# Attention by steps of two query tiles, with the score matmuls of two heads in the two halves of TensorE's rows

## The chip, the cores and the metric

One core of one Trainium2 chip runs the whole program. The metric is the device time of one execution in microseconds, and the time before is the median of 3 runs. TensorE (PE in the profile; PEld is its loading of weights) multiplies, VectorE (DVE), ScalarE (ACT) and GpSimd (POOL) do the elementwise work, and SyncE (SP) issues the DMAs.

## What is computed

Inputs are q, k and v of shape (4, 8, 576, 64): four batches, eight heads, 576 positions, 64 dimensions a head. A small network makes a bias from the distance of two positions. Attention is followed by two MLPs over 2304 tokens.

```python
scores = scale * np.matmul(q, k.transpose(0, 1, 3, 2))
x = (np.log1p(np.abs(rel)) / np.log1p(np.maximum(pos[:, None], 1.0)))[..., None]
bias = np.maximum(x @ w1 + b1, 0.0) @ w2
scores = scores + bias.transpose(2, 0, 1)[None, :, :, :]
scores = scores - np.max(scores, axis=-1, keepdims=True)
attn = np.exp(scores)
attn = attn / (np.sum(attn, axis=-1, keepdims=True) + 1e-09)
out = np.matmul(attn, v)
...
g = h - np.tanh(h)
...
(gate * val) @ w_out
```

## The kernel before

The program has three stages that overlap at their seams: the bias (`bias_phase`, lines 28 to 94), attention (`attention_phase`, lines 127 to 400) and the MLPs (`mlps`, lines 549 to 768). All instructions are put in order by hand: each engine runs its own in the order in which the program's loops emit them.

**Attention** runs over 16 units, a unit being a pair of heads of one batch. A unit has nine query tiles of 128 rows. Tiles 0 to 7 are four blocks of 128 queries, each once for the first head (even tile) and once for the second (odd tile); tile 8 holds the last 64 queries of both heads. The loop at line 333 makes one turn for each tile and works on several tiles at once, at fixed lags: scores of tile t (lag 0), `reduce_min` (lag 1), `expo` (lag 2), `norm` (lag 5), `transposes` (lag 7), `settle` and `settle5` (lag 8).

- `scores` (line 220) multiplies queries with keys. To keep float32 accuracy with the fast format fp32r, each operand is split into a high and a low part. The queries' high part stands in partitions 0 to 63 and their low part in 64 to 127 (`qs`); the keys' high part is there twice, in both halves (`kh`), and their low part likewise (`kl`). So one matmul over all 128 rows gives (qh+ql)·kh and a second (qh+ql)·kl. A tile has 576 scores in each row, in two halves of 288, so it takes four matmuls of 288 columns (line 231). Tile 8 needs both heads' keys and takes ten, since the second head's keys are stored rolled by 64 positions and one half is put together from a piece of 224 and one of 64 columns (`PIECES`, line 122).
- `reduce_min` (line 234, DVE) adds the bias, flips the sign and takes the minimum of each row; it frees the PSUM buffer that `scores` filled. There are two such buffers (line 211), one tile in each.
- `expo` (line 250, ACT) is the exponential with the row's sum, `stats` (line 255, DVE) the reciprocals, `norm` (line 261, POOL) the division.
- `transposes` (line 265, PE) turns a tile by four 128x128 transposes (line 273), with one more for every odd tile (line 277) and, for tile 8, two small matmuls on 64 rows and 64 columns each (lines 281 and 282). `settle` and `settle5` (lines 296 to 308) copy the results to SBUF.
- `pv_steps` (line 310) multiplies with the values for a group of four or five tiles, 256 or 320 columns wide: first two full matmuls (line 320), then sixteen that write 64 output columns of the array each, two heads side by side (line 323). A float32 matmul runs as two instructions. `PV_BURST` (line 404) spreads a group over two of the loop's turns.
- The operands are made by `load_raw`, `high` and `low` (lines 153 to 189): for each unit four raw tiles (queries and keys, each head in a tile of its own, loaded into both partition halves by two DMAs), three casts on ACT and one on DVE, four subtractions and one clearing on POOL. `HIGH` and `LOW` say at which turn.
- `filler` (line 809) puts conversions of the first MLP's weights between, by the table `KIND`; `tail` (line 819) starts the MLPs at the turns in `AT`, counted from the end of the last unit.

In a turn TensorE gets its instructions in this order: the scores of one tile (line 367), the steps of `pv_steps` that are due (lines 371 to 377), the transposes of an earlier tile (line 383). The same functions as the diff touches them follow.

Of the kernel before, what the change touches and what calls it, by code (L numbers as in the profile page):

```python
# [12 lines left out]
ALU = mybir.AluOpType  # L13
# [110 lines left out]
ON_ACT5 = (1, 3, 5, 8)  # L124


def attention_phase(tc, qT, kT, vP, ident_d, par, c_log, bsc, xs, after_bias, load_weight, filler, tail):

# [3 lines left out]
    with ExitStack() as st, ExitStack() as early:  # L132
        right = lambda n, k: st.enter_context(tc.tile_pool(name=n, bufs=k, side="right"))
        vp, np_, sm, xp = right("p1v", 4), right("p1n", NBUF), right("p1m", 3), right("p1x", 2)
# [31 lines left out]
        def alloc(u):  # L166
            prep[u] = (qp.tile([128, 2 * S + 64], F32R, name="qs"), qp.tile([128, 2, S], F32R, name="kh"),
                       qp.tile([128, 2, S], F32R, name="kl"))

        def high(u, i):  # L170
            qs, kh, kl = prep[u]
            a = i // 2
            o = kh[:, a] if i % 2 else qs[:, a * (S + 64):a * (S + 64) + S]
            if i == 3:
                V.tensor_copy(o, raws[u, i])
            else:
                A.copy(o, raws[u, i])

        def low(u, i):
            qs, kh, kl = prep[u]  # L180
            a = i // 2
            r = raws.pop((u, i))
            if i % 2 == 0:
                w = qs[64:128, a * (S + 64):a * (S + 64) + S]
                G.tensor_sub(w, r[64:128], w.bitcast(F32))
                if a == 0:
                    G.memset(qs[:, S:S + 64].bitcast(F32), 0.0)
            else:
                G.tensor_sub(kl[:, a], r, kh[:, a].bitcast(F32))

        def during(k):
            if k < 0:
                alloc(0)
                for i in range(4):
                    load_raw(0, i)
                load_v(0)
                nc.sync.dma_start(ident, ident_d)
            elif 6 <= k < 14 and k % 2 == 0:
                high(0, k // 2 - 3)
            elif 6 <= k < 14:  # L200
                low(0, k // 2 - 3)
# [18 lines left out]
        def scores(u, t):  # L220
            qs, kh, kl = prep[u]
            s = ps_s.tile([128, 2, 512], F32, name="sc")
            if t == 8:
                ops = [(a, qs[:, o:o + 128], k_) for a, o in ((0, 512), (1, S)) for k_ in (kh, kl)]
            else:
                o = t // 2 * 128 + t % 2 * (S + 128)
                ops = [(t % 2, qs[:, o:o + 128], k_) for k_ in (kh, kl)]
            for i, (a, w, k_) in enumerate(ops):
                for hf in range(2):
                    for x, y, n in PIECES[hf] if t == 8 and a else ((0, 288 * hf, 288),):  # L230
                        T.matmul(s[:, hf, x:x + n], w, k_[:, a, y:y + n], start=(i == 0), stop=(i == len(ops) - 1 and x + n == S // 2))  # L231
            sc[u, t] = s

        def reduce_min(u, t):
            s = sc.pop((u, t))
            if t == 8:
                n = np_.tile([128, S], F32, name="n8", bufs=1)
            else:
                if t % 2 == 0:
                    npair[u, t // 2] = np_.tile([128, 2 * S], F32, name="n")  # L240
                n = npair[u, t // 2][:, S * (t % 2):S * (t % 2) + S]
            if t % 3 == 0:
                nmin[u, t // 3] = sm.tile([128, 3], F32, name="mn")
                nsum[u, t // 3] = sm.tile([128, 3], F32, name="sums")
            m = nmin[u, t // 3][:, t % 3:t % 3 + 1]
            V.tensor_tensor_reduce(n.rearrange("p (a b) -> p a b", a=2), s[:, :, 0:288],  # L246
                                   bias[t].rearrange("p (a b) -> p a b", a=2), -0.125, 3.0e38, ALU.add, ALU.min, m)
            ntile[u, t] = n

        def expo(u, t):  # L250
            n = ntile[u, t]
            m = nmin[u, t // 3][:, t % 3:t % 3 + 1]
            A.activation(n, n, AF.Exp, bias=m, scale=-1.0, accum_out=nsum[u, t // 3][:, t % 3:t % 3 + 1])  # L253

        def stats(u, g):
            r = sm.tile([128, 3], F32, name="rec")
            V.tensor_scalar(r, nsum[u, g], 1e-9, None, ALU.add)
            V.reciprocal(r, r)
            nrec[u, g] = r

        def norm(u, t):
            n = ntile[u, t]
            G.tensor_scalar(n, n, nrec[u, t // 3][:, t % 3:t % 3 + 1], 1.0, ALU.mult, ALU.mult)  # L263
# [68 lines left out]
        pvq, late, pv_turn = [], [], 9  # L332
        for tau in range(NU * 9 + TAIL):
            u, t = divmod(tau, 9)
            for _ in range(PER[min(tau, len(PER) - 1)]):
                next(bias_steps, None)
            if tau == LAG - 1:
# [5 lines left out]
            def at_lag(lag):  # L343
                z = tau - lag
                return divmod(z, 9) if 0 <= z < NU * 9 else None
            y = at_lag(2)
            if y:
                expo(*y)
# [3 lines left out]
            y = at_lag(LAG - 2)  # L352
            if y:
                if y[1] % 3 == 0:
                    stats(y[0], y[1] // 3)
                norm(*y)
            z = at_lag(LAG + 1)
            if z:
                settle5(*z)
            y = at_lag(1)  # L360
            if y:
                reduce_min(*y)
                hp, b = units[y[0]]
                if b == NB - 1 and hp + 1 < NP:
                    load_bias(hp + 1, y[1])
            if tau < NU * 9:
                scores(u, t)
            if z:
                settle(*z)
            pv_turn += 1  # L370
            for _ in range(PV_BURST.get(pv_turn, 0)):
                if pvq:
                    f = pvq.pop(0)
                    if f.__name__ == "evac":
                        late.append(f)
                        break
                    f()
            if z and z[1] in (3, 8):
                pvq += pv_steps(z[0], z[1] // 8)
                pv_turn = 0  # L380
            y = at_lag(LAG)
            if y:
                transposes(*y)
            if t == 0 and u + 1 < NU:
                alloc(u + 1)
            if t == 6 and u + 1 < NU:
                load_v(u + 1)
            for n, i in ((u + 1, HIGH.get(t)), (u, HIGH.get(t + 9))):
                if i is not None and 1 <= n < NU:
                    high(n, i)  # L390
            for n, i in ((u + 1, LOW.get(t)), (u, LOW.get(t + 9))):
                if i is not None and 1 <= n < NU:
                    low(n, i)
                    if n + 1 < NU:
                        load_raw(n + 1, i)
            if tau < NU * 9:
                filler(t)
            if tau == NU * 9:
                early.close()
            tail(tau - NU * 9)  # L400


TAIL = 16
PV_BURST = {1: 3, 3: 3}
NBUF = 5
EBUF = 4
LR = (16, 19, 22, 25)
# [3 lines left out]
PER = (2, 2, 2, 2, 2, 2)  # L411
TR = 0
ANY = {t: "AVG" for t in range(9)}
AT = (-4, 1, 3, 7)
KIND = {0: "VV", 2: "V", 4: "VV", 6: "AG", 7: "AG", 8: "AG"}
# [368 lines left out]
def tile_attention_then_two_mlps(ctx: ExitStack, tc: tile.TileContext, qT, kT, vP, par, wi, wo, wg, wv, wo2, c_log, ident, out, xs=None):  # L784
# [6 lines left out]
    with tc.manual_schedule():  # L791
# [17 lines left out]
        def filler(t):  # L809
            for k in KIND.get(t, ""):  # L810
                if not held and W.done < EARLY:
# [29 lines left out]
def _layout(inputs):  # L841
# [6 lines left out]
    def roll(x):  # L848
        return np.concatenate([x[:, :, :64], np.concatenate([x[:, :, 64:, 512:], x[:, :, 64:, :512]], axis=3)], axis=2)
    qt, kt = roll(heads(q)), roll(heads(k))  # L850
# [34 lines left out]
```

## Time and profile before

| | |
|---|---|
| median of 3 runs | 1212.06 us (1210.6 to 1214.28) |
| the profiled execution's own time | 1213.29 us |
| its span in the profile | 1211.5 us |
| TensorE busy | 1181.9 us, 98% of the span |
| DVE, ACT, POOL busy | 725.4, 632.0 and 559.8 us |
| mean granted clock of TensorE | 0.994 of full speed |

The profile is of one execution; its span is the time between its first and its last instruction. In a timeline row the first number is the start in us from the span's start and the second the duration; consecutive instructions of one kind are merged into one row with their count (x4). Matmuls overlap, and their recorded ends are modelled, so what one costs is read from the distance of starts. A form such as 128\*64 gives the rows and columns of the array that a matmul uses; 128x288 behind it is what it writes.

### The profile page before, as it was taken

To read this page: it belongs to the slowest core of one execution; us is meant where nothing else is said; L and a number is where in the kernel's file an instruction comes from. 1 tells how busy PE (TensorE), PEld (TensorE's weight loads), DVE (VectorE), ACT (ScalarE), POOL (GpSimd) and SP (SyncE) were. 2 spreads that over 40 slices of the span, in tenths; PEclk is the share of its full clock that TensorE was granted. 3 is DMA by queue.
4 is the path that set the end of the run, shared out by engine and by line. 5 is a ranking of instruction groups with operands and counts; after the bars stand their busy time and mean duration, and the time that the engine had idled before them with its cause. 6 is when DMAs were issued, how large, how long until landed. Compare 5 with 4: busy or idle time off the path is not lost.

```text
span 1211.5 us, 19227 instructions
## 1 busy us (share of the span) xinstructions
PE 1181.9 (98%) x6992; PEld 1044.7 (86%) x6992; DVE 725.4 (60%) x1253; ACT 632.0 (52%) x1257; POOL 559.8 (46%) x536
## 2 busy tenths in 40 slices
PE   7889999999989999999999999999999999999998
PEld 2247777777769999999999999999999999999997
DVE  7888899999839898898988668862001010010100
ACT  6887888888747767677666556332211211111111
POOL 1039889899735555565555334452221212112111
PEclk9999999999989999999999999999999999999999
DMA  6764848576212333333343322530101001010000
GB/s 195 245 198 141 235 123 230 152 214 171 80 55 79 109 105 123 97 117 122 131 148 105 113 78 81 169 101 9 44 1 40 14 18 35 1 39 14 18 9 26
DMA packets 78894, 120.73 MB, mean 100 GB/s; under 512 B 10064, under 2 KB 53328, under 8 KB 78800
## 3 DMA queue, kind: packets, MB, share of 16 engines
q1 hardware_dynamic: 78800, 119.51, 32.2%
q8 instruction: 55, 0.90, 0.3%
q14 instruction: 39, 0.32, 0.1%
HBM read 89.71 MB, written 29.77 MB: 99 GB/s over the span
## 4 chain that ended last, share of the span: by engine, by line
PE 92%; DMA 2%; DVE 2%; ACT 2%; issue 1%; POOL 0%; SPq 0%; ACTq 0%; DVEq 0%; POOLq 0%
PE up L585 41%; PE acc L662 16%; PE acc L670 12%; PE sc L231 7%; PE pv L323 6%; PE pt L273 6%; PE bt L71 3%; PE pv L320 1%; DMA bsc<-e 1%; PE pf L277 1%; DMA bias<-bsc 1%; DVE y L66 0%; ACT y L64 0%; ACT z L604 0%; PE pf L281 0%
## 5 line engine op out<-in xcount | busy, mean ns | idle before, releaser
L585 PE MATMUL up<-xt,w 128*128 128x384 f32 x2880 | 520.6, 335 | 0.6 <-DVE t L630 0.6
L585 PEld LDWEIGHTS up<-xt,w 128*128 128x128 f32 x2880 | 503.7, 188 | 7.4 <-PE acc L662 0.9
L640 POOL TENSOR_TENSOR gl<-t,gh 128x384 fp32r<-128x384 f32 x168 | 176.1, 1060 | 470.6 <-ACT gh L639 338.4
L632 DVE TENSOR_TENSOR t<-up,t 128x384 f32<-128x384 f32 x72 | 40.1, 557 | 309.2 <-ACT t L611 309.2
L611 ACT ACTIVATE t<-up 128x384 f32<-128x384 f32 x72 | 35.4, 492 | 331.9 <-PE up L585 331.9
L662 PE MATMUL acc<-gh,w 128*128 128x384 f32 x768 | 195.7, 335 | 2.9 <-ACT z L604 2.9
L662 PEld LDWEIGHTS acc<-gh,w 128*128 128x128 f32 x768 | 138.0, 188 | 4.7 <-ACT z L604 3.8
L670 PE MATMUL acc<-w,gh 128*128 128x512 f32 x432 | 134.3, 392 | 0.0
L263 POOL TENSOR_SCALAR n<-n,rec 128x576 f32<-128x576 f32 x144 | 118.2, 832 | 26.3 <-ACT n L253 15.1
L662 PE MATMUL acc<-gl,w 128*128 128x384 f32 x384 | 128.3, 334 | 0.0
L253 ACT ACTIVATE n<-n,mn 128x576 f32<-128x576 f32 x144 | 112.5, 781 | 22.9 <-DVE mn L246 21.8
L246 DVE CUSTOM_DVE_ANT_0 n<-sc,bias 128x576 f32<-128x576 f32 x144 | 107.3, 745 | 23.1 <-PE sc L231 10.4
L571 POOL TENSOR_TENSOR xt<-xm,xt 128x384 fp32r<-128x384 f32 x72 | 73.8, 1040 | 65.9 <-ACT xt L570 65.7
L524 POOL TENSOR_TENSOR w<-wu,w 128x512 fp32r<-128x512 f32 x68 | 97.9, 1443 | 7.2 <-ACT w L526 6.1
L670 PEld LDWEIGHTS acc<-w,gh 128*128 128x128 f32 x432 | 80.1, 188 | 13.5
L273 PE MATMUL pt<-ident,n 128*128 128x128 f32 x576 | 90.6, 280 | 0.0
L273 PEld LDWEIGHTS pt<-ident,n 128*128 128x128 f32 x576 | 66.4, 142 | 27.6 <-POOL n L263 7.8
L639 ACT CAST gh<-t 128x384 fp32r<-128x384 f32 x168 | 84.8, 511 | 8.4 <-PE acc L662 3.6
L625 ACT ACTIVATE z<-z,c 128x768 f32<-128x768 f32 x48 | 45.2, 941 | 77.7 <-DVE up L624 77.7
L670 PE MATMUL acc<-w,gl 128*128 128x512 f32 x216 | 85.4, 395 | 0.0
L231 PE MATMUL sc<-kh,qs 128*128 128x288 f32 x336 | 81.4, 327 | 3.8 <-DVE mn L246 3.7
L626 DVE TENSOR_TENSOR t<-up,t 128x768 f32<-128x768 f32 x48 | 45.9, 957 | 60.9 <-ACT t L604 60.8
(70 smaller groups left out, 1696.3 us busy)
## 6 DMA issues: line engine op xcount, KB each, us to landing
wraw<-in_wo SPq DMA_DIRECT2D x28, 512.0 KB, 3.7
bsc<-e SPq DMA_DIRECT2D x36, 295.5 KB, 3.0
raw<-in_qT SPq DMA_DIRECT2D x64, 144.0 KB, 3.9
raw<-in_kT SPq DMA_DIRECT2D x64, 144.0 KB, 2.8
xm<-xs SPq DMA_DIRECT2D x48, 192.0 KB, 3.6
x2s<-o SPq DMA_DIRECT2D x48, 192.0 KB, 3.7
wraw<-in_wi SPq DMA_DIRECT2D x16, 512.0 KB, 4.2
wraw<-in_wg SPq DMA_DIRECT2D x12, 512.0 KB, 3.7
```

What stands on the lines that cost most here:

```text
L231: T.matmul(s[:, hf, x:x + n], w, k_[:, a, y:y + n], start=(i == 0), stop=(i == len(ops) - 1 and x + n == S // 2))
L246: V.tensor_tensor_reduce(n.rearrange("p (a b) -> p a b", a=2), s[:, :, 0:288], bias[t].rearrange("p (a b) -> p a b", a=2), -0.125, 3.0e38, ...
L253: A.activation(n, n, AF.Exp, bias=m, scale=-1.0, accum_out=nsum[u, t // 3][:, t % 3:t % 3 + 1])
L263: G.tensor_scalar(n, n, nrec[u, t // 3][:, t % 3:t % 3 + 1], 1.0, ALU.mult, ALU.mult)
L273: T.transpose(pt[:, i], n[:, o:o + 128], ident)
L524: self.nc.gpsimd.tensor_sub(w[:, 1], u, w[:, 0].bitcast(F32))
L571: G.tensor_sub(t[:, 1], m, t[:, 0].bitcast(F32))
L585: T.matmul(p[:, 0:TB], w[:, a, 128 * kt:128 * kt + 128], x[:, c], start=(kt == 0 and i == 0), stop=(kt == 3 and i == 2))
L639: A.copy(h, x[:, j])
L640: G.tensor_sub(l, x[:, j], h.bitcast(F32))
L662: T.matmul(ac[blk][d][:, 0:TB], w[:, a, 128 * d:128 * d + 128], c, start=(begin and j == 0 and i == 0), stop=(end and j == NPR - 1 and i = ...
L670: T.matmul(ac[blk][d], g[:, c], w[:, a], start=(begin and i == 0), stop=(end and i == 2))
```

## The change

The loop makes five turns (steps) for a unit instead of nine: four of two tiles (one block of queries, both heads) and one for tile 8 alone. The queries and keys of both heads stand in one tile each, the first head in partitions 0 to 63 and the second in 64 to 127, with separate tiles for high and low parts. The scores are now three products, qh·kh, ql·kh and qh·kl, over 64 rows for each head; the matmuls of the two heads are issued alternately and address the two halves of the array's rows. The rolled order of the second head's keys is now made by the matmuls: its first half takes a piece of 64 and a piece of 224 columns (`ROLL`). For tile 8 the host puts the last 64 queries of both heads into a block-diagonal 128x128 tile, so one set of six matmuls over all 128 rows does it. In a step TensorE's order is now scores, transposes, values.

```diff
-LAG = 7
 NU = NP * NB
-HIGH = {1: 0, 3: 1, 5: 2, 7: 3}
-LOW = {2: 0, 4: 1, 6: 2, 8: 3}
+STEP_TILES = ((0, 1), (2, 3), (4, 5), (6, 7), (8,))
+NS = len(STEP_TILES)
+PREP = {0: ("high", 0), 1: ("high", 1), 2: ("low", 0), 3: ("low", 1)}
+GROUP = (0, 0, 1, 1, 2)
 GW = (256, 320)
-PIECES = ((0, 64, 288),), ((0, 352, 224), (224, 0, 64))
+QK = (S + 64, S)
+ROLL = ((0, 512, 64), (64, 0, 224)), ((0, 224, 288),)
...
         def load_raw(u, i):
             hp, b = units[u]
-            src, a = ((qT, 0), (kT, 0), (qT, 1), (kT, 1))[i]
-            r = stg.tile([128, S], F32, name=f"raw{i}")
-            for o in (0, 64):
-                nc.sync.dma_start(r[o:o + 64], src[b, hp, 64 * a:64 * a + 64])
+            r = stg.tile([128, QK[i]], F32, name=f"raw{i}")
+            nc.sync.dma_start(r, (qT, kT)[i][b, hp])
             raws[u, i] = r
...
         def high(u, i):
...
+            A.copy(prep[u][i][0], raws[u, i])
 
         def low(u, i):
...
+            h, l = prep[u][i]
+            G.tensor_sub(l, raws.pop((u, i)), h.bitcast(F32))
...
-        def scores(u, t):
...
+        def scores(u, s):
+            (qh, ql), (kh, kl) = prep[u]
+            tiles = STEP_TILES[s]
+            for t in tiles:
+                sc[u, t] = ps_s.tile([128, 2, 512], F32, name="sc")
+            for i, (q, k) in enumerate(((qh, kh), (ql, kh), (qh, kl))):
                 for hf in range(2):
...
+                    for a, t in enumerate(tiles):
+                        r = slice(0, 128) if t == 8 else slice(64 * a, 64 * a + 64)
+                        for x, y, n in ROLL[hf] if a else ((0, 288 * hf, 288),):
+                            T.matmul(sc[u, t][:, hf, x:x + n], q[r, 128 * s:128 * s + 128], k[r, y:y + n],
+                                     start=(i == 0 and x == 0), stop=(i == 2 and x + n == S // 2))
...
         def settle5(u, t):
             if t in (1, 3, 5, 8):
                 o = place5(at[u, min(t // 4, 1)][1], t)
-                (A.copy if t in ON_ACT5 else V.tensor_copy)(o, tf.pop((u, t))[:, 0:o.shape[1]])
+                A.copy(o, tf.pop((u, t))[:, 0:o.shape[1]])
...
+        for sg in range(NU * NS + TAIL):
+            u, s = divmod(sg, NS)
+            for _ in range(PER):
                 next(bias_steps, None)
...
             for f in late:
                 f()
             late = []
+            z = at_lag(5)
+            if z:
+                for t in STEP_TILES[z[1]]:
+                    settle5(z[0], t)
+                for t in STEP_TILES[z[1]]:
+                    settle(z[0], t)
+            if sg < NU * NS:
+                filler(s, "V")
+            y = at_lag(2)
+            if y and y[1] in (1, 3, 4):
+                stats(y[0], GROUP[y[1]])
+            y = at_lag(3)
             if y:
+                for t in STEP_TILES[y[1]]:
+                    norm(y[0], t)
             y = at_lag(1)
             if y:
+                for t in STEP_TILES[y[1]]:
+                    expo(y[0], t)
+            if sg < NU * NS:
+                scores(u, s)
+                hp, b = units[u]
+                for t in STEP_TILES[s]:
+                    reduce_min(u, t)
+                    if b == NB - 1 and hp + 1 < NP:
+                        load_bias(hp + 1, t)
+            y = at_lag(4)
+            if y:
+                for t in STEP_TILES[y[1]]:
+                    transposes(y[0], t)
+            if z and z[1] in (1, 4):
+                pvq += pv_steps(z[0], z[1] // 4)
+            for _ in range(PVN[s] if sg < NU * NS + 4 else 5):
                 if pvq:
+                    pvq.pop(0)()
+                    if pvq and pvq[0].__name__ == "evac":
+                        late.append(pvq.pop(0))
                         break
...
+            if s in PREP and 1 <= u + 1 < NU:
+                k, i = PREP[s]
+                if k == "high":
+                    high(u + 1, i)
+                else:
+                    low(u + 1, i)
+                    if u + 2 < NU:
+                        load_raw(u + 2, i)
+            if sg < NU * NS:
+                filler(s, "AG")
...
-PV_BURST = {1: 3, 3: 3}
+TAIL = 9
+PVN = (2, 1, 3, 2, 2)
...
-LR = (16, 19, 22, 25)
+LR = (16, 19)
...
-PER = (2, 2, 2, 2, 2, 2)
+PER = 4
...
-AT = (-4, 1, 3, 7)
-KIND = {0: "VV", 2: "V", 4: "VV", 6: "AG", 7: "AG", 8: "AG"}
+AT = (-2, 1, 2, 4)
+KIND = {0: "AGA", 1: "V", 2: "V", 4: "VV"}
...
-    qt, kt = roll(heads(q)), roll(heads(k))
+    qt, kt = heads(q), heads(k)
+    tail = np.zeros((NB, NP, 128, 128), np.float32)
+    for a in range(2):
+        tail[:, :, 64 * a:64 * a + 64, 64 * a:64 * a + 64] = qt[:, :, 64 * a:64 * a + 64, 512:]
+    qt = np.concatenate([qt[..., :512], tail], axis=3)
```

## Rows read from the trace of the kernel before

**Rows 1.** The page's busy times, and its slices of the granted clock.
```profile
PE 1181.9 (98%) x6992; PEld 1044.7 (86%) x6992; DVE 725.4 (60%) x1253; ACT 632.0 (52%) x1257; POOL 559.8 (46%) x536
...
PEclk9999999999989999999999999999999999999999
```

**Rows 2.** Busy time by engine in one unit: stretch, PE, PEld, DVE, ACT, POOL, PEclk, DMA.
```profile
206.33:222.67 16.34, 16.34 (x125) 12.47 (x123) 15.05 (x36) 13.43 (x34) 14.82 (x16) 1.00 0.69 186
```

**Rows 3.** Timeline of PE in that unit: scores, transposes, values, scores again.
```profile
209.01 0.60 PE L273 MATMUL pt<-ident,n 128*128 128x128 f32 x4
209.36 0.51 PE L231 MATMUL sc<-kh,qs 128*128 128x288 f32 x2
209.71 0.42 PE L231 MATMUL sc<-kl,qs 128*128 128x288 f32 x2
210.06 1.08 PE L323 MATMUL pv<-at,vs 128*64 128x256 f32 x8
211.08 0.66 PE L273 MATMUL pt<-ident,n 128*128 128x128 f32 x4
...
212.20 0.60 PE L273 MATMUL pt<-ident,n 128*128 128x128 f32 x4
212.73 0.27 PE L281 MATMUL pf<-ident,n 64*64 64x64 f32 x1
212.74 0.27 PE L282 MATMUL pf<-ident,n 64*64 64x64 f32 x1
...
212.99 0.53 PE L231 MATMUL sc<-kh,qs 128*128 128x288 f32 x2
213.36 0.43 PE L231 MATMUL sc<-kl,qs 128*128 128x288 f32 x2
```

**Rows 4.** The same timeline: tile 8's second head, then the wide group of values.
```profile
214.33 0.42 PE L231 MATMUL sc<-kl,qs 128*128 128x288 f32 x2
214.59 0.43 PE L231 MATMUL sc<-kh,qs 128*128 128x288 f32 x3
214.86 0.52 PE L231 MATMUL sc<-kl,qs 128*128 128x288 f32 x3
215.22 0.78 PE L320 MATMUL pv<-a,vs 128*128 128x320 f32 x2
215.93 1.30 PE L323 MATMUL pv<-at,vs 128*64 128x320 f32 x8
217.16 0.66 PE L273 MATMUL pt<-ident,n 128*128 128x128 f32 x4
217.65 0.27 PE L277 MATMUL pf<-ident,n 128*128 128x128 f32 x1
```

**Rows 5.** Timeline of PE in the tail: eight pairs of values without a break.
```profile
356.45 2.37 PE L323 MATMUL pv<-at,vs 128*64 128x320 f32 x16
358.75 4.43 PE L585 MATMUL up<-xt,w 128*128 128x384 f32 x24
```

**Rows 6.** Groups of instructions by shape: out<-in, count, busy us, mean ns, idle before.
```profile
L246 DVE CUSTOM_DVE_ANT_0 n<-sc,bias 128x576 f32<-128x576 f32 x144 | 107.3, 745 | 23.1 <-PE sc L231 10.4 <-POOL n L263 9.6 <-DMA bias<-bsc 3.0
...
L185 POOL TENSOR_TENSOR qs<-raw,qs 64x576 fp32r<-64x576 f32 x32 | 49.9, 1560 | 57.2 <-ACT qs L177 51.8 <-issue 3.0
...
L189 POOL TENSOR_TENSOR kl<-raw,kh 128x576 fp32r<-128x576 f32 x32 | 45.5, 1423 | 13.4 <-ACT kh L177 10.2 <-DVE kh L175 3.2
...
L177 ACT CAST qs<-raw 128x576 fp32r<-128x576 f32 x32 | 21.4, 668 | 0.0
...
L175 DVE CAST kh<-raw 128x576 fp32r<-128x576 f32 x16 | 11.4, 711 | 0.0
```

**Rows 7.** DMA issues of the page: count, KB each, us to landing.
```profile
raw<-in_qT SPq DMA_DIRECT2D x64, 144.0 KB, 3.9
```

**Rows 8.** The seams: PE in the first unit, and PE behind the last scores.
```profile
87.46 0.50 PE L231 MATMUL sc<-kh,qs 128*128 128x288 f32 x2 [2.68 <-DVE mn L246]
...
340.01 1.22 PE L320 MATMUL pv<-a,vs 128*128 128x256 f32 x2 [4.91 <-ACT a L308]
```

More of the change, by code (lines that the diff above doesn't have):

```diff
@@ L166, in alloc @@
         def alloc(u):
-            prep[u] = (qp.tile([128, 2 * S + 64], F32R, name="qs"), qp.tile([128, 2, S], F32R, name="kh"),
-                       qp.tile([128, 2, S], F32R, name="kl"))
+            prep[u] = [[qp.tile([128, QK[i]], F32R, name="qk"[i] + y) for y in "hl"] for i in range(2)]
         def high(u, i):
[L171 to L177, printed above, removed]
-        def low(u, i):
[L180 to L189, printed above, removed]
+            A.copy(prep[u][i][0], raws[u, i])
+        def low(u, i):
+            h, l = prep[u][i]
+            G.tensor_sub(l, raws.pop((u, i)), h.bitcast(F32))
         def during(k):
@@ L193, in during @@
                 alloc(0)
-                for i in range(4):
+                for i in range(2):
                     load_raw(0, i)
@@ L197, in during @@
                 nc.sync.dma_start(ident, ident_d)
[L198 to L201, printed above, removed]
+            elif 6 <= k < 10:
+                (low if k % 2 else high)(0, k // 2 - 3)
             if k in LR:
@@ L241, in reduce_min @@
                 n = npair[u, t // 2][:, S * (t % 2):S * (t % 2) + S]
[L242 to L245, printed above, removed]
+            if t % 4 == 0:
+                nmin[u, t // 4] = sm.tile([128, 4], F32, name="mn")
+                nsum[u, t // 4] = sm.tile([128, 4], F32, name="sums")
+            m = nmin[u, t // 4][:, t % 4:t % 4 + 1]
             V.tensor_tensor_reduce(n.rearrange("p (a b) -> p a b", a=2), s[:, :, 0:288],
@@ L251, in expo @@
             n = ntile[u, t]
-            m = nmin[u, t // 3][:, t % 3:t % 3 + 1]
-            A.activation(n, n, AF.Exp, bias=m, scale=-1.0, accum_out=nsum[u, t // 3][:, t % 3:t % 3 + 1])
+            m = nmin[u, t // 4][:, t % 4:t % 4 + 1]
+            A.activation(n, n, AF.Exp, bias=m, scale=-1.0, accum_out=nsum[u, t // 4][:, t % 4:t % 4 + 1])
         def stats(u, g):
-            r = sm.tile([128, 3], F32, name="rec")
-            V.tensor_scalar(r, nsum[u, g], 1e-9, None, ALU.add)
-            V.reciprocal(r, r)
+            w = 1 if g == 2 else 4
+            r = sm.tile([128, 4], F32, name="rec")
+            V.tensor_scalar(r[:, 0:w], nsum[u, g][:, 0:w], 1e-9, None, ALU.add)
+            V.reciprocal(r[:, 0:w], r[:, 0:w])
             nrec[u, g] = r
@@ L262, in norm @@
             n = ntile[u, t]
[L263 removed]
+            G.tensor_scalar(n, n, nrec[u, t // 4][:, t % 4:t % 4 + 1], 1.0, ALU.mult, ALU.mult)
         def transposes(u, t):
@@ L330, in pv_steps @@
             return [lambda c=c: mm(c) for c in range(5)] + [evac]
[L332 to L335, printed above, removed]
+        pvq, late = [], []
+        for sg in range(NU * NS + TAIL):
+            u, s = divmod(sg, NS)
+            for _ in range(PER):
                 next(bias_steps, None)
-            if tau == LAG - 1:
+            if sg == 3:
                 assert next(bias_steps, 1) == 1
@@ L343, in at_lag @@
             def at_lag(lag):
[L344 to L348, printed above, removed]
+                z = sg - lag
+                return divmod(z, NS) if 0 <= z < NU * NS else None
             for f in late:
@@ L360, in attention_phase @@
+            y = at_lag(2)
+            if y and y[1] in (1, 3, 4):
+                stats(y[0], GROUP[y[1]])
+            y = at_lag(3)
+            if y:
+                for t in STEP_TILES[y[1]]:
+                    norm(y[0], t)
             y = at_lag(1)
             if y:
[L362 to L371, printed above, removed]
+                for t in STEP_TILES[y[1]]:
[8 more added lines that the diff above has]
+            y = at_lag(4)
@@ L376, in attention_phase @@
                         break
[L377 to L384, printed above, removed]
+            if s == 0 and u + 1 < NU:
                 alloc(u + 1)
-            if t == 6 and u + 1 < NU:
+            if s == 3 and u + 1 < NU:
                 load_v(u + 1)
-            for n, i in ((u + 1, HIGH.get(t)), (u, HIGH.get(t + 9))):
-                if i is not None and 1 <= n < NU:
-                    high(n, i)
@@ L391, in attention_phase @@
[L391 to L398, printed above, removed]
+            if s in PREP and 1 <= u + 1 < NU:
[6 more added lines that the diff above has]
+                        load_raw(u + 2, i)
@@ L399, in attention_phase @@
+            if sg < NU * NS:
+                filler(s, "AG")
+            if sg == NU * NS:
                 early.close()
-            tail(tau - NU * 9)
-TAIL = 16
-PV_BURST = {1: 3, 3: 3}
+            tail(sg - NU * NS)
+TAIL = 9
+PVN = (2, 1, 3, 2, 2)
 NBUF = 5
 EBUF = 4
-LR = (16, 19, 22, 25)
+LR = (16, 19)
 LW = (3, 4)
@@ L410 @@
 ALONE = 28
-PER = (2, 2, 2, 2, 2, 2)
+PER = 4
 TR = 0
-ANY = {t: "AVG" for t in range(9)}
-AT = (-4, 1, 3, 7)
-KIND = {0: "VV", 2: "V", 4: "VV", 6: "AG", 7: "AG", 8: "AG"}
+AT = (-2, 1, 2, 4)
+KIND = {0: "AGA", 1: "V", 2: "V", 4: "VV"}
 TBS = (None, 384, 384)
@@ L807, in after_bias, with filler @@
             W.open(ctx.enter_context(tc.tile_pool(name="wa", bufs=1)), 0, EARLY)
-        def filler(t):
+        def filler(t, kinds):
             for k in KIND.get(t, ""):
+                if k not in kinds:
+                    continue
                 if not held and W.done < EARLY:
```

26 lines of the change are left out of this document (1 added, 25 removed).

## The prediction

> **What bounds the kernel now.** I read the page first, then the busy time of one unit, then that unit's timeline on TensorE, matmul by matmul. The page says that TensorE is busy for 98% of the span at full clock [rows 1]. That alone is weak, as recorded ends are modelled. The unit is better evidence: cut from one start of its first value matmul to the next, it lasts 16.34 us, TensorE has no hole in it, and DVE, ACT and POOL are busy for 15.05, 13.43 and 14.82 us [rows 2]. So attention, 16 units, is paced by the distances between TensorE's instructions, and the other engines have 1.3 us a unit or more to spare. What counts is what TensorE's list costs before and after, and whether another engine gets in its way.
>
> **Prices on TensorE**, all from distances of starts. Two score matmuls take 214.59 - 214.33 = 0.26 us, 0.13 each for 288 columns [rows 4]. Four transposes and two score matmuls take 0.70, so a transpose takes 0.11 [rows 3]. Tile 8's second head comes as 288, 224 and 64 columns. Its two trios take 0.63, and the next instructions start 0.08 late (0.71 instead of two full value matmuls at 0.27 and an entry of 0.09, below), so a trio costs 0.355 [rows 4]. By columns it should cost 0.26, what two halves of 288 take. The small piece is too short to cover the load of the weights behind it: 0.355 less 0.13 leaves 0.112 for each of the two pieces, whatever their width.
>
> Eight pairs of 320-column value matmuls take 2.30 [rows 5], four pairs with the way out take 1.23 [rows 4], hence 0.268 a pair: as much as one full matmul, so two column halves do run side by side. The two small matmuls on different rows and columns start 0.01 apart [rows 3].
>
> A change of form costs time. Going from scores to values adds 0.35 - 0.26 = 0.09, inside and on the way out 1.23 - 1.07 = 0.16 are lost, and the first transposes are late by 0.49 - 0.44 = 0.05 [rows 3, 4]. So there and back costs 0.30. I split this as about 0.10 for emptying the array at each change plus the first weight load that nothing covers: 0.05 into values or transposes. Into scores that load is 0.11, as they show behind the small matmuls (0.37 instead of 0.26). The small matmuls' own excursion costs 0.09 + 0.26 + 0.11 less about 0.10 of work, so 0.36 [rows 3].
>
> **The change, part by part, in a unit.**
>
> Scores. Before: eight tiles at 4 x 0.13 = 0.52, and tile 8 at 0.52 + 0.71, together 5.39. After, a step of two tiles makes three products; in each the first head streams 2 x 288 columns, the second 64, 224 and 288. No row shows 64-row matmuls of one form side by side. The lower end is 0.26 a product (both heads together, pieces free). The upper end is five loads one after the other, 5 x 0.112 = 0.56. I take the two heads side by side, as the column halves and the small matmuls run, but the second head at the trio's 0.355, the row of the same three widths. Four steps then cost 12 x 0.355 = 4.26, tile 8 takes 6 x 0.13 = 0.78, together 5.04. Gain 0.35.
>
> Changes of form. Before there are four excursions to the values and one to the small matmuls: 4 x 0.30 + 0.36 = 1.56. After, every two-tile step goes scores (row halves), transposes (full), values (column halves) and back: the values, which stood in four bursts, now run in all five steps, and scores no longer share a form with transposes. Into row-half scores 4 x (0.10 + 0.11) = 0.84; from them to transposes 4 x 0.16 = 0.64; into values from a full form 4 x 0.145 = 0.58; small matmuls in and on to the values 0.30; values to tile 8's full scores 0.21. Sum 2.57, loss 1.01. No row shows a change into or out of row halves; bounds are 0 for the emptying and double my price, and I take the price of the changes that are shown.
>
> Transposes and value matmuls stay as they are. TensorE per unit: -0.35 + 1.01 = **+0.66 us**, times 16 units +10.6 us.
>
> Preparation of queries and keys. POOL loses 2 x 1.56 + 2 x 1.42 = 5.97 us and gets about 1.42 + 1.58 = 3.0 (576 and 640 columns on 128 partitions); ACT's three casts of 0.67 become two (1.4 us); DVE loses one of 0.71 [rows 6]. SP issues two raw loads a unit, not eight of 144 KB [rows 7]. All this ran under TensorE and still does: 0. Would TensorE stop being the bound, these are what gives room.
>
> Waits. A step fills both score buffers, so its scores wait until DVE has reduced the two tiles before. From that release: load 0.11, three products 1.07, about 0.16 until the last result is out, two reductions 2 x 0.745 + 0.08 [rows 6], together 2.9 us. TensorE's own five steps take by the prices above 3.6, 3.1, 3.85, 3.15 and 3.2 us. The wait ends first, with 0.2 us left in the tightest: 0, but close. In front of the reductions DVE has up to 2.4 us of copies and weight conversion (step 4), behind which TensorE's next scores would stand. The fillers convert one weight a unit, four steps on DVE, two on ACT, one on POOL, as needed: 0, hidden.
>
> Seams. In the first unit TensorE waits 2.68 us for a reduction that needs the last bias; behind the last scores it waits 4.91 us behind ACT, whose queue holds the MLP's first inputs [rows 8]. Both causes stay. Scores run one tile less ahead at the first, at most one turn, 16.34 / 9 = 1.8 us; the tail's order moves by less than a turn. I take 0, with 2 us to either side.
>
> Sum: the profiled execution's 1213.3 + 10.6 = 1223.9. The median is 1.2 below that execution, so **1222.5**.
>
> **Rivals.**
>
> *The pieces are free.* If weights load fast enough in each row half, or ahead by more than one, a product takes 0.26. Then 12 x 0.095 = 1.14 us go, the unit is 0.48 shorter, 7.7 us in all: **1204.5**. Against it speaks the trio [rows 4]; for it, that loads for the small matmuls in different row halves run at once [rows 3]. It decides as soon as the second head's three pieces take under 0.30. The Trainium skill, TensorEngine Tiling (Array Packing), section "Theoretical Speedup", promises up to twice the rate for 64 rows; that is this rival, and no run before shows row tiles of this kind.
>
> *Row halves need no emptying.* If only columns matter for a change of form, the 0.64 behind the scores goes and the rest nearly cancels (+0.02): **1212.5**, no change. For it: no row shows the price. Against: all changes that are shown cost the same 0.09 to 0.10.
>
> *Two buffers in lockstep.* If release and restart or DVE's list take 0.3 us more a step than I have, TensorE waits: 5 x 0.3 = 1.5 us a unit, 24 us more: **1246.5**. For it: only 0.2 us of slack. Against: DVE has less to do than before.
>
> *The halves don't help each other.* If the five loads of a product queue, it takes 0.56, 12 x 0.205 = 2.46 us a unit, 39 us more: **1262**. Then the change doesn't do what it says. Against: the small matmuls' loads. The Trainium skill, TensorE: Matmul & The Clock Gate, Part 3, "The mechanism", says that a load overlaps a running matmul only where the row group differs; that would expose the second head's three loads and give nearly this time. The trace speaks against so strict a reading: the full-array scores, always on the same rows, follow each other every 0.13 us [rows 4].
>
> **How the numbers follow.** About 0.3% is what a measurement of this kernel can tell from no change. Chances: forecast 0.46 (1217 to 1228), free pieces 0.22 (1200 to 1208), no emptying 0.14 (1208 to 1217), lockstep 0.10, queueing loads 0.08. Faster: nearly all of the second and a fifth of the third, 0.24. Same: most of the third, 0.10. Slower: the rest, 0.66. The range of 1202 to 1240 leaves out the queueing loads, half of the lockstep and the lower third of the free pieces, 0.20 together.
>
> **What would show it.** Right: a unit of 17.0 us with TensorE again without holes; in the form 64\*128 a product of five matmuls every 0.355 us; first transposes some 0.16 us late behind the row halves. Wrong: products every 0.26 (free pieces) or 0.56 (queueing loads); score matmuls waiting for DVE's minimum in each step (lockstep); transposes following row-half scores without a gap.

## The result, and the profile after

The changed kernel takes **1219.59 us** (median of five runs, 1217.87 to 1221.7) against 1212.06: a ratio of 1.0063, interval 1.0046 to 1.0079, so slower by 7.5 us where 10.4 were forecast. Its profiled execution took 1219.56 us with a span of 1217.5.

The page after, busy times and the loads of queries and keys, against [rows 1, 7]:

```profile
PE 1192.4 (98%) x7376; PEld 1042.0 (86%) x7376; DVE 694.9 (57%) x1237; ACT 621.5 (51%) x1241; POOL 503.1 (41%) x488
...
raw<-in_qT SPq DMA_DIRECT2D x16, 320.0 KB, 3.4
```

Three engines and SP have less to do, and TensorE has 10.5 us more. One unit by engine, to be held against [rows 2]: a stretch as long as the distance from one start of a value matmul to the same one a unit later (stretch, PE, PEld, DVE, ACT, POOL, granted clock, DMA share, GB/s):

```profile
205.00:221.89 16.89, 16.89 (x148) 12.20 (x147) 12.88 (x35) 12.79 (x33) 11.30 (x13) 1.00 0.47 152
```

The unit went from 16.34 to 16.89 us, and TensorE is again without a hole at full clock, while DVE, ACT and POOL lost 2.17, 0.64 and 3.52 us. The unit follows TensorE, whose list got longer; that the others have less to do did not make it shorter. Where in the unit the time goes is read from its timeline, to be held against [rows 3, 4] (start, duration, engine, line, operation, out<-in, form, shape, count; a row that merges matmuls of 288, 224 and 64 columns shows the shape of its first):

```profile
209.66 0.62 PE L213 MATMUL sc<-kh,qh 64*128 64x288 f32 x5
...
211.96 0.60 PE L303 MATMUL pv<-a,vs 128*128 128x256 f32 x2
...
213.51 0.62 PE L213 MATMUL sc<-kh,qh 64*128 64x288 f32 x5
213.88 0.47 PE L213 MATMUL sc<-kh,ql 64*128 64x288 f32 x4
214.14 0.29 PE L213 MATMUL sc<-kl,qh 64*128 64x288 f32 x1
214.18 0.30 PE L213 MATMUL sc<-kh,ql 64*128 64x288 f32 x1
214.27 0.57 PE L213 MATMUL sc<-kl,qh 64*128 64x288 f32 x4
214.77 0.66 PE L256 MATMUL pt<-ident,n 128*128 128x128 f32 x4
...
215.47 0.22 PE L265 MATMUL pf<-ident,n 64*64 64x64 f32 x1
215.62 1.08 PE L306 MATMUL pv<-at,vs 128*64 128x256 f32 x8
216.63 0.54 PE L213 MATMUL sc<-kh,qh 128*128 128x288 f32 x2
...
219.84 0.62 PE L213 MATMUL sc<-kh,qh 64*128 64x288 f32 x5
220.21 0.47 PE L213 MATMUL sc<-kh,ql 64*128 64x288 f32 x4
```

From the first row-half score to the transposes behind, 214.77 - 213.51 = 1.26 us: three products at the forecast's 0.355 and 0.195 more for the change of form. The steps begin at 209.66, 213.51, 216.63 and 219.84, so they take 3.85, 3.12 and 3.21 us; the forecast had 3.85, 3.15 and 3.2.

The units in the middle are alike, each in its kernel. Between the second unit's value matmul and the fifteenth's lie 13 units. Before, those two matmuls start at 108.29 and 320.71:

```profile
108.29 0.38 PE L320 MATMUL pv<-a,vs 128*128 128x256 f32 x1
...
320.71 0.38 PE L320 MATMUL pv<-a,vs 128*128 128x256 f32 x1
```

After, at 110.64 and 330.17:

```profile
110.64 0.38 PE L303 MATMUL pv<-a,vs 128*128 128x256 f32 x1
...
330.17 0.38 PE L303 MATMUL pv<-a,vs 128*128 128x256 f32 x1
```

212.42 us became 219.53: +7.11, or 0.547 a unit. The span grew by 6.0 (1211.5 to 1217.5), so everything outside these 13 units gave back 1.1. Little of that lies at the end. The last scores of attention start here, before and after:

```profile
329.24 0.52 PE L231 MATMUL sc<-kl,qs 128*128 128x288 f32 x3
```

```profile
335.48 0.43 PE L213 MATMUL sc<-kl,qh 128*128 128x288 f32 x2
```

From there to the end of the span it is 1211.5 - 329.24 = 882.3 us before and 1217.5 - 335.48 = 882.0 after.

What the forecast named as the signs of being wrong is absent inside the units. The chains of waits between 108 and 325 us (engine and tile, what ended the wait: us in total, times, longest) have no row of PE itself. First a row of the kernel before, then three of the changed one:

```profile
DVE n L246 <- PE sc L231: 7.0, 9, 1.2
...
POOL n L246 <- DVE rec L241: 70.2, 25, 3.3
DVE n L228 <- PE sc L213: 43.4, 48, 1.5
...
PEld sc L213 <- DVE mn L228: 11.4, 26, 0.5
```

DVE now waits for TensorE, 43.4 us where before it was 7.0. Only weight loads wait for DVE's minimum, at most 0.5 us, behind value matmuls that still run: a sign of how near the lockstep is.

### The profile page after: what moved, and what is told of

The parts are those of the page before. It is cut to its first block, busy times and chain, and to the rows that moved or that the text cites. A ratio compares the mean times of both kernels' runs of the same rounds, so it can differ in the third digit from the quotient of the medians.

```text
span 1217.5 us, 19642 instructions
## 1 busy us (share of the span) xinstructions
PE 1192.4 (98%) x7376; PEld 1042.0 (86%) x7376; DVE 694.9 (57%) x1237; ACT 621.5 (51%) x1241; POOL 503.1 (41%) x488
## 4 chain that ended last, share of the span: by engine, by line
PE 94%; DVE 2%; ACT 1%; issue 1%; DMA 1%; POOL 0%; SPq 0%; ACTq 0%; POOLq 0%; DVEq 0%
PE up L570 41%; PE acc L647 15%; PE acc L655 12%; PE sc L213 8%; PE pv L306 6%; PE pt L256 6%; PE bt L71 4%; PE pv L303 1%; PE pf L260 1%; DMA lg<-in_c_log 0%; DVE n L228 0%; DVE y L66 0%; ACT z L589 0%; PE pf L264 0%; DMA wraw<-in_wv 0%
## 5 line engine op out<-in xcount | busy, mean ns | idle before, releaser
L246 POOL TENSOR_SCALAR n<-n,rec 128x576 f32<-128x576 f32 x144 | 114.8, 811 | 102.2 <-DVE rec L241 97.1
L228 DVE CUSTOM_DVE_ANT_0 n<-sc,bias 128x576 f32<-128x576 f32 x144 | 103.8, 754 | 55.5 <-PE sc L213 54.9
L256 PE MATMUL pt<-ident,n 128*128 128x128 f32 x576 | 80.5, 281 | 1.8 <-DVE at L286 1.8
L306 PE MATMUL pv<-at,vs 128*64 128x320 f32 (+1 forms) x512 | 80.2, 425 | 0.0
L256 PEld LDWEIGHTS pt<-ident,n 128*128 128x128 f32 x576 | 63.4, 141 | 12.1 <-issue 1.8
```

Of the source, the lines that this page charges most:

```text
L246: G.tensor_scalar(n, n, nrec[u, t // 4][:, t % 4:t % 4 + 1], 1.0, ALU.mult, ALU.mult)
L256: T.transpose(pt[:, i], n[:, o:o + 128], ident)
L306: T.matmul(p[0][64 * a:64 * a + 64, 0:N], v[:, c - 1, a], main[:, c - 1, a * N:a * N + N], start=False, stop=(c == 4))
```

## The experiments

Theory: a unit is the length of TensorE's list; the two small pieces of the second head cost 0.112 us each whatever their width, and each change of the array's form about 0.15. The rivals: lockstep of the score buffers, the seams, and that the other engines are more in the way than their busy time says.

**Keys in one piece** (on the changed kernel). The host puts the keys' last 64 columns once more in front of them, so both heads stream 288 columns in a row.

```
-QK = (S + 64, S)
-ROLL = ((0, 512, 64), (64, 0, 224)), ((0, 224, 288),)
+QK = (S + 64, S + 64)
...
+                        y = 288 * hf + 64 * (1 - a)
+                        T.matmul(sc[u, t][:, hf, 0:288], q[r, 128 * s:128 * s + 128], k[r, y:y + 288], ...)
...
+    kt = np.concatenate([kt[..., 512:], kt], axis=3)
```

> Theory (TensorE's list of instructions is the time; the second head's pieces of 64 and 224 columns set the length of a product): with the keys loaded with their last 64 columns once more in front, each half of the second head is one matmul of 288 columns, so a product falls from 0.355 to 0.26 us. Twelve products a unit, 1.14 us: the unit goes from 16.89 to about 15.75 us, the time from 1219.6 to about 1202.5. Rival (the two score buffers that a step fills, and DVE behind them, set the pace): the products get shorter but TensorE then waits for DVE's minimum; the unit stays at 16.5 us or more, the time above 1213. Second rival (the loads of weights of the two row halves queue, 0.112 each): a product takes 4 x 0.112 = 0.45 and the time rises.

Measured: 1202.97 us (1201.15 to 1204.17), ratio to the kernel before 0.9927 [0.9911, 0.9942]. Its unit, and one step's scores on TensorE:

```profile
205.00:220.78 15.78, 15.78 (x138) 10.99 (x136) 13.24 (x34) 12.76 (x33) 11.93 (x13) 1.00 0.39 116
```

```profile
210.31 0.53 PE L212 MATMUL sc<-kh,qh 64*128 64x288 f32 x4
210.68 0.42 PE L212 MATMUL sc<-kh,ql 64*128 64x288 f32 x4
210.94 0.43 PE L212 MATMUL sc<-kl,qh 64*128 64x288 f32 x4
211.30 1.09 PE L255 MATMUL pt<-ident,n 128*128 128x128 f32 x8
```

A product of both heads takes 210.94 - 210.68 = 0.26 us, the time of two full-row matmuls. The scores in row halves do run at twice the rate, as the Trainium skill has it in TensorEngine Tiling (Array Packing), "Theoretical Speedup" ("Up to 2×"), but only once no piece is narrow. Twelve products in a unit lost 0.095 each: 1.14 forecast, 16.89 - 15.78 = 1.11 measured in most units (three of the 13 in the middle are longer, 15.96 to 16.16 us). The pieces were the cost of the change, and without them it is a gain.

**One more change of form** (on the changed kernel). In the four two-tile steps the odd tile's transposes go behind the values.

```
-                for t in STEP_TILES[y[1]]:
+                for t in STEP_TILES[y[1]][:1]:
                     transposes(y[0], t)
...
+            if y:
+                for t in STEP_TILES[y[1]][1:]:
+                    transposes(y[0], t)
```

> The odd tile's transposes move behind the values, so that in four steps of a unit TensorE goes to the full form once more. Theory (a change of form costs 0.10 us for emptying the array and the first load of weights): four more changes of 0.155 us, 0.62 us a unit, unit 17.5 us, time about 1229. Rival (changes of form are hidden, and the loss of the change lies in the pieces alone): within 2 us of 1219.6.

Measured: 1228.13 us (1227.84 to 1230.36), ratio 1.014 [1.012, 1.0159]. Its unit, then a step on TensorE:

```profile
205.00:222.47 17.47, 17.47 (x147) 12.12 (x146) 14.21 (x35) 12.88 (x33) 11.43 (x12) 1.00 0.51 165
```

```profile
205.13 0.76 PE L306 MATMUL pv<-at,vs 128*64 128x320 f32 x4
205.82 0.66 PE L256 MATMUL pt<-ident,n 128*128 128x128 f32 x4
206.31 0.27 PE L260 MATMUL pf<-ident,n 128*128 128x128 f32 x1
206.52 0.62 PE L213 MATMUL sc<-kh,qh 64*128 64x288 f32 x5
```

The same work in the same shapes, with four changes more: 17.47 - 16.89 = 0.58, or 0.145 each, where 0.155 was expected.

**Values in two steps** (on the changed kernel). The ten steps of value matmuls of a unit run in two of the five steps instead of in all; this takes changes of form away, and takes from three steps the work that runs while DVE reduces.

```
-PVN = (2, 1, 3, 2, 2)
+PVN = (5, 0, 5, 0, 0)
```

> All values of a group run in one step, two excursions a unit in place of five. Theory of forms alone: three changes fewer, 0.45 us a unit, time about 1213. With the two score buffers counted: steps without values are shorter on TensorE (2.0 to 2.4 us) than from the release of the buffers to their next release (2.9 us, and 3.2 in the step where DVE converts weights), so TensorE waits for DVE's minimum some 2.5 us a unit: unit about 18.9 us, time about 1250. If the buffers never bind, 1213.

Measured: 1240.74 us (1240.45 to 1240.95), ratio 1.0239 [1.0217, 1.0261]. Its unit, a step without values on TensorE, and PE's waits between 108 and 325 us:

```profile
205.00:223.30 18.30, 17.41 (x148) 12.80 (x146) 12.65 (x35) 12.81 (x33) 10.89 (x12) 1.00 0.64 197
```

```profile
211.41 0.40 PE L213 MATMUL sc<-kh,qh 64*128 64x288 f32 x1
212.65 0.48 PE L213 MATMUL sc<-kh,qh 64*128 64x64 f32 x3 [0.85 <-DVE mn L228]
```

```profile
PE sc L213 <- DVE mn L228: 10.2, 12, 0.9
```

The first head starts on its free buffer, the second stands 1.24 us for the other. The direction is the lockstep's: fewer changes of form, and yet 1.41 us more a unit, of which 18.30 - 17.41 = 0.89 is an open hole (the other 0.52 isn't traced to its place here). The size was put some 10 us too high. So the values that now run in each step cost changes of form and are the cover for DVE's two reductions as well.

**The bias earlier** (on the kernel before). Four steps of the bias instead of two are taken per turn of attention's start, as in the changed kernel per step of two tiles, to see what an earlier start is worth.

```
-PER = (2, 2, 2, 2, 2, 2)
+PER = (4, 4, 4, 4, 4, 4)
```

> The kernel before with one edit: four bias steps a turn instead of two while attention starts, as many as the changed kernel runs in a step. Theory (the changed kernel wins back about 2 us at the start because its bias ends earlier and the first unit's last reduction waits less): the last bias matmul comes 2 us earlier, the wait of 2.68 us for the minimum shrinks, time about 1210. Rival (what was won back comes from fewer loads and casts of queries and keys during the bias): no difference, 1212, or slower as four steps stand in front of one tile's scores.

Measured: 1211.06 us (1210.2 to 1212.07) against 1211.85, ratio 0.9996 [0.9987, 1.0005]: no difference that can be told. In its trace attention does get going earlier: the last bias matmul comes at 73.77 instead of 76.19 and the first value matmul at 89.24 instead of 91.79. The longest wait in the first unit, 2.68 us [rows 8], is now

```profile
79.72 0.53 PE L231 MATMUL sc<-kh,qs 128*128 128x288 f32 x2 [1.41 <-DVE mn L246]
```

and the unit stays 16.34; the waits for reductions in the first unit add up to 3.50 us, 3.73 before. One profile's start moved by over 2 us, the median by less than 1. Inconclusive for the start, and a bound: by the interval an earlier bias is worth at most 0.0013 x 1212 = 1.6 us.

**Keys in one piece, on the kernel before.** If the pieces are all that matters, the kernel before can also be rid of its two trios a unit without row halves. Both heads' keys get the 64 columns; one buffer fewer in the bias stage pays for the room.

```
-PIECES = ((0, 64, 288),), ((0, 352, 224), (224, 0, 64))
...
-            r = stg.tile([128, S], F32, name=f"raw{i}")
+            r = stg.tile([128, S + 64 * (i % 2)], F32, name=f"raw{i}")
...
-EBUF = 4
+EBUF = 3
...
```

> The kernel before with keys that carry their last 64 columns once more in front, so that tile 8's second head needs four matmuls of 288 instead of six in pieces (one buffer of the bias stage is given up for the room). It tells how much of the gain of the version with row halves and whole keys is the keys alone. Theory: two trios of 0.355 become 2 x 0.26, 0.19 us a unit, unit 16.15 us, 3 us less, about 1209; so of the 9 us between 1212 and 1203, some 6 are the row halves'. Rival (POOL, whose two subtractions get 64 columns more, takes over as the bound): unit stays at 16.34 us, time 1212. If the bias stage misses its buffer, the first score matmul comes later and the unit is still 16.15.

A miss: 1218.81 us (1217.6 to 1221.75) against 1212.83, ratio 1.0061 [1.004, 1.0081]. POOL's subtractions got wider (group by shape, against [rows 6]: count, busy us, mean ns, idle before):

```profile
L188 POOL TENSOR_TENSOR kl<-raw,kh 128x640 fp32r<-128x640 f32 x32 | 49.9, 1560 | 13.4 <-ACT kh L176 10.2 <-DVE kh L174 3.2
```

That is 2 x 0.14 = 0.27 us more a unit for an engine that had 14.82 of 16.34 busy, and TensorE's unit comes out at 16.53 to 16.74 instead of the 16.15 expected: on its timeline transposes that begin at 206.90 are followed by scores only at 207.55, 0.30 later than the same pair in [rows 3]. What the scores wait for stands on the load of their weights:

```profile
204.07 0.30 PEld L230 LDWEIGHTS sc<-kl,qs 128*128 128x128 f32 x2 [0.17 <-POOL kl L188]
...
207.55 0.30 PEld L230 LDWEIGHTS sc<-kh,qs 128*128 128x128 f32 x2 [0.29 <-DVE mn L245]
```

The larger one is for the reduction on DVE that frees a score buffer, the smaller one for POOL's low part of the keys; the kernel before has neither in these 13 units. So time taken off TensorE's list was lost to DVE and POOL; whether DVE was late by its own wider cast or by POOL's wider subtractions isn't separated. The "1.3 us to spare" of the forecast was not free to be used. (The buffer taken away belongs to the bias stage; the next run lacks it too, and its unit is shorter than before.)

**The same with less preparation** (on the kernel before). Only the second head's keys get the columns, its cast goes from DVE to ACT.

```
...
+            w = S + 64 * (i == 3)
...
-            if i == 3:
-                V.tensor_copy(o, raws[u, i])
-            else:
-                A.copy(o, raws[u, i])
+            A.copy(o, raws[u, i])
...
+                    y = S * a + 288 * hf + 64 * (t == 8 and a)
...
```

> The run before it (the kernel before, whole keys) missed: its unit went to 16.62 us, 0.28 more, just what its two subtractions on POOL grew by (2 x 0.14), and DVE's cast grew too. Here only the second head's keys get the 64 extra columns (0.14 us on POOL) and the second head's cast of the keys goes from DVE to ACT, which frees 0.7 us of DVE. Theory (TensorE's list is 16.15 us; the path over POOL and DVE sat close under TensorE's 16.34 and the run before lifted it over): unit between 16.15 and 16.3 us, time 1209 to 1211.5. Rival (POOL alone sets it): unit 16.34 + 0.14 = 16.48, time 1214. If 16.15 comes out, the row halves with whole keys are worth 0.37 us a unit over full rows with whole keys.

Measured: 1212.61 us (1209.0 to 1215.04) against 1212.63, ratio 0.9996 [0.9985, 1.0008]. The unit came out as worked out:

```profile
205.00:221.16 16.16, 16.16 (x122) 12.29 (x120) 14.09 (x35) 13.89 (x35) 14.87 (x15) 1.00 0.79 213
```

16.34 - 16.16 = 0.18 us less. The time did not follow: the last bias matmul comes at 78.76 instead of 76.19 and the first value matmul at 93.59 instead of 91.79, and 1.8 us later eats most of 16 x 0.18 = 2.9. This run too has one buffer fewer in the bias stage, and whether that or the longer cast makes it late isn't separated. A miss on the time, and the comparison that the change deserves: with whole keys on both sides, the rest of the change is worth 16.16 - 15.78 = 0.38 us a unit. That rest is the row halves together with the order by steps and the shorter preparation; no run has the row halves alone.

**No form of their own** (the first experiment, and tile 8's two small products taken over all 128 rows, with 64 columns of the identity that pick the rows wanted).

```
-                T.matmul(pf[0:64, 128:192], n[0:64, 512:S], ident[0:64, 0:64], start=True, stop=True)
-                T.matmul(pf[64:128, 128:192], n[64:128, 512:S], ident[64:128, 64:128], start=True, stop=True)
+                T.matmul(pf[0:64, 128:192], n[:, 512:S], ident[:, 0:64], start=True, stop=True)
+                T.matmul(pf[64:128, 128:192], n[:, 512:S], ident[:, 64:128], start=True, stop=True)
```

> The version with the keys in one piece (1203.0), and tile 8's two small matmuls written with all 128 rows and 64 columns, the form of the values that follow them, in place of 64 rows and 64 columns. Theory of forms: one change fewer a unit, 0.15 us, unit 15.78 to about 15.63 us, time about 1200.5. Rival (the emptying is paid by any two neighbours of different operands, not by the form): unit stays at 15.78 us, time 1203.

Measured: 1201.04 us (1200.18 to 1201.22), ratio 0.9905 [0.9886, 0.9925], the shortest time of all. On TensorE's timeline:

```profile
206.16 0.22 PE L264 MATMUL pf<-ident,n 128*64 128x64 f32 x1
206.21 1.04 PE L305 MATMUL pv<-at,vs 128*64 128x256 f32 x8
```

The values, now of the same form, follow the small matmuls after 0.05 us; in the changed kernel they follow after 215.62 - 215.47 = 0.15. Of that tenth the unit shows half: most are 15.73 against 15.78, the shortest 15.64. Where the rest went is open. The ratio's interval overlaps the first experiment's, so this second step is likely but not sure.

**Preparation doubled** (on the changed kernel). Each of POOL's two subtractions a unit is made a second time.

```
-            G.tensor_sub(l, raws.pop((u, i)), h.bitcast(F32))
+            r = raws.pop((u, i))
+            G.tensor_sub(l, r, h.bitcast(F32))
+            G.tensor_sub(stg.tile([128, QK[i]], F32, name="spare"), r, h.bitcast(F32))
```

> The changed kernel with each of POOL's two subtractions of the preparation done twice, the second into a tile that nobody reads: POOL gets back the 3.0 us a unit that the change took from it. Theory (preparation lies under TensorE and is worth nothing by itself): unit stays at 16.89 us, time within 2 us of 1219.6. Rival (POOL's path was as long as TensorE's in the kernel before, and the shorter preparation is part of what the change gains): unit above 17.2 us, time above 1224.

Measured: 1227.12 us (1226.7 to 1231.66), ratio 1.013 [1.0113, 1.0148]; the unit is 17.23. The rival won: 0.34 us a unit, and 16 of them are 5.4 of the 7.5 us between the medians. POOL, though busy for 11.30 us of 16.89 in the changed kernel, could not take 3.0 us for nothing. DVE's timeline in the changed kernel, around a weight conversion (L495) ahead of tile 8's reduction (L228):

```profile
216.87 0.74 DVE L495 SCALAR_TENSOR_TENSOR wu<-wraw,wu 128x512 int32<-128x512 int32 x1
217.65 1.12 DVE L491 SCALAR_TENSOR_TENSOR wu<-wraw,wu 128x512 int32<-128x512 int32 x1
218.69 0.74 DVE L228 CUSTOM_DVE_ANT_0 n<-sc,bias 128x576 f32<-128x576 f32 x1
```

With the preparation doubled, the same stretch on DVE, with POOL's and TensorE's rows of that time:

```profile
209.37 1.42 DVE L497 SCALAR_TENSOR_TENSOR wu<-wraw,wu 128x512 int32<-128x512 int32 x1
210.82 1.13 DVE L493 SCALAR_TENSOR_TENSOR wu<-wraw,wu 128x512 int32<-128x512 int32 x1
211.87 0.74 DVE L230 CUSTOM_DVE_ANT_0 n<-sc,bias 128x576 f32<-128x576 f32 x1
```

```profile
208.80 1.44 POOL L176 TENSOR_TENSOR spare<-raw,kh 128x576 f32<-128x576 f32 x1
```

```profile
212.32 0.83 PE L215 MATMUL sc<-kh,qh 64*128 64x288 f32 x4
212.92 0.29 PE L215 MATMUL sc<-kh,ql 64*128 64x288 f32 x1
...
216.29 0.62 PE L215 MATMUL sc<-kh,qh 64*128 64x288 f32 x5
```

The conversion starts while POOL subtracts and takes 1.42 us instead of 0.74; the reduction behind it starts 2.50 us after the conversion's start instead of 1.82; and the second product, 0.37 behind the first in the same step of the changed kernel (220.21 - 219.84), comes 0.60 behind. The reduction ends at 211.87 + 0.74 = 212.61, later than the first head's scores begin (212.32): the second head, whose buffer it frees, stands for it. The whole loss lies in this step, the first of a unit: it takes 216.29 - 212.32 = 3.97 us where the changed kernel takes 223.47 - 219.84 = 3.63, and the other four keep their lengths to 0.02. So work on POOL reaches TensorE by way of DVE. The Trainium skill, SBUF — State Buffer, section "SBUF: two separate sides", calls the ports that DVE and GpSimd share "an exclusive lock" for an operation of DVE with two SBUF inputs against a GpSimd one that reads SBUF. The conversion has two such inputs, and that it takes longer agrees. A conversion held until POOL's subtraction ends (208.80 + 1.44 = 210.24) would have taken 0.87 + 0.74 = 1.61 us and not 1.42, with POOL's times rough; that the lock is the cause is an inference from times that coincide.

## Why the prediction was right or wrong

**The bound**: right. The unit follows the length of TensorE's list in the changed kernel and in the first two experiments; where cover was taken away (values in two steps), work was added (preparation doubled) or there was no room (whole keys on the kernel before), TensorE waited for DVE's reduction, and in the last of these for POOL too.

**Scores**: right. The second head's trio sets a product at 0.355; taking the pieces away gives 0.26. "The pieces are free" and "the halves don't help each other" are both out: it is neither 0.26 nor 0.56, and in the first experiment it is 0.26 for both heads together. With it falls the strict reading of the rule on row groups in the Trainium skill, TensorE: Matmul & The Clock Gate, Part 3, "The mechanism", that the prediction weighed.

**Changes of form**: right. Behind the row halves 0.195 against the 0.16 taken, an added change 0.145 against the same. "Row halves need no emptying" is out. What the array does in that time no run shows; its price is what is measured.

**The sum in a unit**: the direction and most of the size, +0.55 against +0.66. The step that was mis-sized is "TensorE per unit: -0.35 + 1.01". Its two lists were never added up and held against the unit that was known. Before: scores 5.39, changes 1.56, 40 transposes at 0.11 are 4.40, values 4.82, the small matmuls' own work 0.10, together 16.27, where [rows 2] has 16.34. After: 5.04, 2.57 and the same rest, 16.93, where 16.89 was measured. Before was 0.07 too short and after 0.04 too long; the difference of two lists of 16 us carries both. The forecast had the better number at hand: its own five steps under "Waits" add up to 16.9. Which price made the list of before too short stays open. The rows give 0.01 us, and a price taken from two of them is used up to 40 times in a unit: 0.002 us more for each of the 36 full-row score matmuls would already be 0.07.

**Times 16, and the seams**: 13 whole units gave 7.11. The forecast's +0.66 for the other three, with seams at 0 to 2 either way, allowed 0 to +4.0 there; it was -1.1, outside. At the end nothing came of it: the wait of 4.91 us [rows 8] is gone from behind the last scores and four of 0.69 to 1.09, 3.55 us in all, stand there instead, and the time from the last scores to the end is the same to 0.3 us. So most of the difference lies at the start. There the last bias matmul comes 2.8 us earlier (73.37 instead of 76.19); the waits for reductions in the first unit are five, 2.63 us in all, where before they were four with 3.73 (0.68, 0.15, 0.22 and the 2.68 of [rows 8]). Neither is shown to be the cause: the run with the bias earlier told nothing of it, and five runs of the kernel before alone lie 3.7 us apart, so that 1.1 between two profiles may be chance. The step from profile to median hid a part too: before, the median is 1.2 below the profiled execution, after they are equal, which is how a span 6.0 longer makes 7.5 between medians.

**Preparation: 0**: right for what it was used for, as no engine but TensorE set the unit after. But it was not idle work: "would TensorE stop being the bound, these are what gives room" is the better half of the sentence. Putting the 3.0 us back on POOL, at this place in its list, costs 0.34 a unit, nearly the 0.38 that the change is worth once keys are whole on both sides. The slack was read from busy time, and the run on the kernel before with wider keys shows that busy time overstated it.

**Lockstep**: right that it ends first, with little to spare. Two experiments that take that little away pay at once, +1.41 and +0.34 us a unit.

## What to carry to other kernels

A matmul streamed in pieces can cost more than its columns: here a product of 64, 224 and 288 columns took 0.355 us, and 0.26 as two of 288. The forecast's reading, that a short piece doesn't cover the load of the weights behind it, carried the size from the kernel before to the changed one. Before work is split to pack the array, see that each piece stays wide; storing 64 columns twice turned +7 us into -9. Count the changes of the array's form per step as instructions with a price of their own, add the priced list up, and hold it against the measured period before taking a difference of two such lists. And test slack by doing the hidden work twice: an engine with a third of the unit idle was still tied to the bound through another engine's reduction.

## What the runs showed that was not expected

- The two row halves don't keep the program's order. In the timeline after, the first head's third product starts (214.14, kl with qh) before the last matmul of the second product (214.18, kh with ql), which stands ahead of it in the program: by the records each half goes through its own matmuls, the first head at about 0.26 a product (214.14 - 213.88), and only the second at 0.355.
- A head's first matmul starts alone when only its buffer is free: 1.24 us ahead of the other in the run with values in two steps.
- Where a subtraction on POOL ran beside a conversion on DVE with which it shares no tile, DVE's took 0.68 us longer, 1.42 instead of 0.74.
